# Attention followed by a ResMLP block: the first batch's pass takes the schedule of the later passes

## The chip, the cores and the metric

The kernel runs on one core of one Trainium2 chip. The metric is the device time of one execution in microseconds (us); the number given for a kernel is the median of its runs. PE is TensorE, DVE is VectorE, ACT is ScalarE, POOL is GpSimd and SP is SyncE; Pool and SP issue most of the DMAs, each on a queue of its own.

## What is computed

```python
B, Hq, Hkv, S, D = 8, 16, 4, 384, 64          # DM = Hq * D = 1024, DFF = 4096
k, v = repeat(k, 4), repeat(v, 4)             # four query heads share one k and v head
attn = softmax(q @ k.T / sqrt(D)) @ v         # [B, Hq, S, D]
x    = attn.transpose(0, 2, 1, 3).reshape(B, S, DM)
a1   = alpha1 * x + beta1
tok  = einsum('ts,bsd->btd', w_tok, a1)       # mixes the tokens of one batch
u    = x + lam * tok
a2   = alpha2 * u + beta2
ch   = relu(a2 @ w_ch1) @ w_ch2               # 1024 -> 4096 -> 1024
out  = u + lam * ch                           # float32, [8, 384, 1024]
```

Inputs and output are float32; the matmuls run in bf16 and accumulate in float32.

## The kernel before

The kernel goes through the eight batches one after the other. For each it has two kinds of work. The *side work* of a batch is everything up to `a2`: attention, token mixing, and the transposes that bring `a2` into `a2T`, which has the features on the partitions. The *pass* of a batch (`main`) is its MLP. During the pass of batch b, the side work of batch b + 1 is put between the matmuls of the MLP, so that PE always has something to do. The order on each engine is the order in which the program writes the instructions; nothing is reordered.

**The pass.** `main(b)` has two halves. The first half computes `hT`, 32 tiles of 128 hidden features (`nt` 0 to 31): each is eight matmuls `h` (L439, 128x128 by 384 columns, 385 in batch 0, where an extra column carries the bias) into one of two PSUM banks tagged "mm", and then an evacuation with ReLU, on ACT for even `nt` and on DVE for odd ones (L447, L449; in batch 0 a copy of the bias column goes ahead, L445). W1 does not stay in SBUF: it is loaded again in every pass in 16 chunks of two `nt` each (`load_w1`, L133, Pool's queue), into a ring of five buffers, so that the load of chunk c + 5 is issued when chunk c has been used. The second half computes six output tiles of 32 matmuls `ch` each (L474, 512 columns): first the three row tiles for the left 512 columns, then the three for the right ones. DVE multiplies by `lam` and adds the residual (L479, L480, two operations), and SP stores the tile (L481). W2 does stay in SBUF and is loaded once, in the first pass (`load_w2`, L138). The left half's first 16 `nt` are one load of 2048 KB that stands ahead of everything in `main`; the second quarter of W2, `nt` 16 to 31 of the left half, and the whole right half follow during the first pass.

**Yields and turns.** `main` is a generator. It yields in the middle and at the end of every `nt` of the first half (at the end only for the first four `nt` of batch 0, whose matmuls run ahead of the pass, in `h_part`), and after every four `ch` matmuls of the second half, 48 times. What the loop over the batches does at a yield is called a turn here.

In the passes of batches 1 to 6 `side(b + 1)` returns a table from a turn's number to what is issued there. Turns are counted from the last yield of the first half on, so turn 0 comes ahead of the first `ch` matmul. `scores3` computes three banks of scores (12 matmuls, L214) and their exponentials on ACT (L223); `av` multiplies by v for one pair of heads (18 matmuls, L257), after which DVE normalises and makes `a1` (L262, L263, L270, L272); `tok_flip` mixes tokens for the same 128 features (9 matmuls, L278), adds the residual and scales on DVE (L285, L289), and transposes the result into `a2T` with a DMA transpose on SP's queue (L301). Scores, av and tok share three PSUM slots of two banks each (`threes`). Turns 34 to 43 of these passes also carry the DMA transposes of the batch after: `flip_k` (L118) for `kT`, and `flip_q` (L122) for two pairs of heads at a time, four calls in all.

In the pass of batch 0, `side(1)` returns a list, and a rule on the time passed spreads its entries evenly over both halves. There the side work uses other PSUM pools: two slots for scores, one bank "av", one bank "tp". Scores are done in pairs of banks (`scores2`), and av in halves (`av_piece`). k and q of batch 1 are transposed on PE (`k_transpose`, L189; `q_transpose`, L200; DVE copies them out), and the rows of vectors h1, al2 and lam_t are spread over the partitions by matmuls (`spread`, L344, copied by ACT, L346) after DVE has split them into bf16 parts (`split`). The `a2` blocks of the first six pairs of heads go through DMA transposes, the last two through PE and ACT (L307, L310). At three quarters of the pass `flip_k(2)` and a single `flip_q(2)` for all heads are issued.

**Queues.** Pool's queue carries q, v, W1 and W2 in the order of the program; a load on it waits in its issue until the load eight places ahead has landed. Ahead of the first pass it has chunks 0 to 4 of W1, q and v of batch 1, and the first quarter of W2. SP's queue carries the stores, the loads of k and all DMA transposes, also in the order of the program.

The first pass before, as the loop sets it:

```python
for dt in main(b):
    t += dt
    if b == 0:
        ...
        if done < len(us) and done * t_all * 0.82 < len(us) * (t - t_all * 0.04):
            us[done]()
            done += 1
        if not flipped and t > t_all * 0.75:
            flipped = True
            flip_k(2)
            flip_q(2)
    elif t >= 2 * NNT * T_H:
        for f, *a in us.get(u, []):
            f(*a)
        u += 1
```

Of the kernel before, what the change touches and what calls it, by code (L numbers as in the profile page):

```python
# [12 lines left out]
def kernel(  # L13
# [157 lines left out]
    def side(b):  # L171
# [34 lines left out]
        def scores(i, later=False):  # L206
            sc = bank([P, 2, 4, P], "sc", "sc") if b < 2 else three()
            k = 4 * i
            while k < 4 * i + 4:
                n = min(4 * i + 4, k - k % NST + NST) - k  # L210
                p, sk, st = k // (NST * NST), k // NST % NST, k % NST
                for hh in range(2):
                    r = slice(hh * D, (hh + 1) * D)
                    nc.tensor.matmul(out=sc[:, hh, k % 4:k % 4 + n], lhsT=kT[r, sk, 2 * p // G, :],  # L214
                                     rhs=qT[r, p, st:st + n, :], start=True, stop=True)
                k += n

            def exp():
                if first:
                    e = hTf[:, i % 6 * 1024:(i % 6 + 1) * 1024].rearrange("p (h k s) -> p h k s", h=2, k=4)  # L220
                else:
                    e = sb.tile([P, 2, 4, P], bf, tag="es", name="es", bufs=EB)
                nc.scalar.activation(out=e, in_=sc, func=EXP, scale=scale_qk)  # L223
                ess[i] = e

            if later:
                late.append(exp)
            else:
                exp()

        def scores2(j):
            while late:
                late.pop(0)()
            scores(2 * j)
            scores(2 * j + 1, True)


# [4 lines left out]
        def av_piece(p, hh):  # L242
            while late and b < 2:
                late.pop(0)()
            if hh == 0:
                if b < 2:
                    avs[p] = bank([P, 2, NST, D1], "mm" if first else "av", "av")
                else:
                    avs[p] = three()[:, 0].rearrange("p k s -> p (k s)")[:, :2 * NST * D1].rearrange(
                        "p (h st d) -> p h st d", h=2, st=NST)  # L250
# [23 lines left out]
        def tok(p):  # L274
            ps = bank([P, NST, P], "mm" if first else "av", "tok") if b < 2 else three()[:, 0, :NST]
            for tt in range(NST):
# [14 lines left out]
        def a2_transpose(p):  # L291
            if first:
                ps = bank([P, NST, P], "tp" if p % 2 else "av", "ut")
                for tt in range(NST):
                    nc.tensor.matmul(out=ps[:, tt, :], lhsT=x[:, tt, cols(p)], rhs=ident_f, is_transpose=True,  # L295
                                     start=(tt == 0), stop=(tt == NST - 1), skip_group_check=True)
                nc.scalar.activation(out=a2T[:, p, :S], in_=ps.rearrange("p a b -> p (a b)"),
                                     func=mybir.ActivationFunctionType.Copy, scale=al2T[:, p:p + 1])
                return
            if b > 1 or p < 6:  # L300
                nc.sync.dma_start_transpose(  # L301
                    out=a2T[:, p, :S].rearrange("p (a s) -> p a s", a=NST),
                    in_=a2s[p].rearrange("p a d -> p (a d)"))
                return
            ps = tp_ps([P, NST, P])
            for tt in range(NST):
                nc.tensor.matmul(out=ps[:, tt, :], lhsT=a2s[p][:, tt, :], rhs=ident,  # L307
                                 is_transpose=True, start=(tt == 0), stop=(tt == NST - 1),
                                 skip_group_check=True)
            nc.scalar.copy(out=a2T[:, p, :S], in_=ps.rearrange("p a b -> p (a b)"))  # L310

# [42 lines left out]
        def av(p):  # L354
            av_piece(p, 0)
            av_piece(p, 1)
            if b > 1:
                while late:
                    late.pop(0)()

# [3 lines left out]

        if b > 1:

            return {0: [(scores3, 0)], 4: [(av, 0)], 6: [(scores3, 1)], 8: [(tok_flip, 0)], 11: [(av, 1)],
                    13: [(scores3, 2, True)], 15: [(av, 2)], 16: [(tok_flip, 1)], 18: [(tok_flip, 2)], 19: [(av, 3)],
                    21: [(scores3, 3)], 23: [(tok_flip, 3)], 25: [(av, 4)], 27: [(scores3, 4)], 29: [(tok_flip, 4)],
                    31: [(av, 5)], 33: [(scores3, 5, True)], 35: [(av, 6), (tok_flip, 5)], 37: [(av, 7)],  # L370
                    39: [(tok_flip, 6)], 41: [(tok_flip, 7)]}
        if not first:
            add(split, 2, 4)
            add(k_transpose, 0)
            add(q_transpose, 0, 2, "av")
            add(k_transpose, 2)
            add(q_transpose, 2, 2, "av")
            for j in range(NP + 4):
                if 1 < j < NP + 2:
                    add(av_piece, j - 2, 0)  # L380
                    add(av_piece, j - 2, 1)
                if j <= NP:
                    add(scores2, j)
                    if j in (1, 3):
                        add(q_transpose, 4 + 2 * (j // 2))
                if 2 < j < NP + 3:
                    add(tok, j - 3)
                if j > 3:
                    add(a2_transpose, j - 4)
                if j < 2:  # L390
                    for p in (4 * j, 4 * j + 2):
                        add(spread, (p, p + 1), (1, 3), "tp", "ACT")
                    add(spread, range(4 * j, 4 * j + 4), (3, 4), "tp", "ACT")
            return us
        add(k_transpose, 0, 1)
# [29 lines left out]

    T_H, T_C = 4 * S, 4 * 512

    def main(b):
# [3 lines left out]
        for c in range(NCH):  # L432
            w1 = w1_tiles.pop(b * NCH + c)
            for j in range(CW):
# [3 lines left out]
                for dt in range(0 if begun else NDT):  # L438
                    nc.tensor.matmul(out=ps[:, :n], lhsT=w1[:, dt, j * P:(j + 1) * P],  # L439
                                     rhs=a2T[:, dt, :n], start=(dt == 0), stop=(dt == NDT - 1))  # L440
                    if dt == 3:
                        yield T_H
                c1 = bias1[:, nt:nt + 1]
# [4 lines left out]
                else:  # L448
                    nc.vector.tensor_scalar(out=hT[:, nt, :], in0=ps[:, :S], scalar1=c1,  # L449
                                            scalar2=0.0, op0=ADD, op1=mybir.AluOpType.max)  # L450
                yield T_H

            if b or c + RING < NCH:
                load_w1(b * NCH + c + RING)
            if b == 0 and c in (3, 5, 7, 9):
                load_w2(0, 8 + c // 2 - 1, 16)
            if b == 0 and c == NCH - RING:
                for i in (6, 7):
                    load_w2(0, i, 8)
                for i in range(8):  # L460
# [5 lines left out]
        for dw in range(NDW):  # L466
            cs = slice(dw * 512, (dw + 1) * 512)
            for ms in range(NST):
# [3 lines left out]
                for lo, hi in ((0, 256), (256, 384), (384, 512)) if last else ((0, 512),):  # L472
                    for nt in range(NNT):
                        nc.tensor.matmul(out=ps[:, lo:hi], lhsT=hT[:, nt, ms * P:(ms + 1) * P],  # L474
                                         rhs=w2[:, nt, dw * 512 + lo:dw * 512 + hi], start=(nt == 0), stop=(nt == NNT - 1))
                        if nt % 4 == 3 and nt < NNT - 1:
                            yield T_C
                    c = slice(dw * 512 + lo, dw * 512 + hi)
                    nc.vector.tensor_tensor(out=o[:, lo:hi], in0=ps[:, lo:hi], in1=lam_t[:, c], op=MUL)  # L479
                    nc.vector.tensor_tensor(out=o[:, lo:hi], in0=o[:, lo:hi], in1=x[:, ms, c], op=ADD)  # L480
                    nc.sync.dma_start(out=out[b].rearrange("(p st) d -> p st d", st=NST)[:, ms, c], in_=o[:, lo:hi])  # L481
                yield T_C

    t_all = 2 * NNT * T_H + 8 * NST * NDW * T_C
    order = {mybir.EngineType.PE, mybir.EngineType.DVE, mybir.EngineType.Activation,
             mybir.EngineType.Pool, mybir.EngineType.SP}
    with tc.manual_schedule(engines=order):
# [99 lines left out]
        place_k(1, 0)  # L587
        place_k(1, 1)
        for b in range(B):
            us = side(b + 1) if b + 1 < B else {}  # L590
            half = False
            done, t = 0, 0
            if b == 0:
                load_k(2)
            elif b + 2 < B:
                for u, f, *a in ((1, load_k), (2, load_next), (34, flip_k), (36, flip_q, 0, 2), (37, flip_q, 2, 2),
                                 (42, flip_q, 4, 2), (43, flip_q, 6, 2)):
                    us.setdefault(u, []).append((f, b + 2, *a))
            flipped = False
            u = 0  # L600
            for dt in main(b):
                t += dt
                if b == 0:
                    half = not half
                    if late and half:
                        late.pop(0)()
                    if done < len(us) and done * t_all * 0.82 < len(us) * (t - t_all * 0.04):
                        us[done]()
                        done += 1
                    if not flipped and t > t_all * 0.75:  # L610
                        flipped = True
                        flip_k(2)
                        flip_q(2)
                elif t >= 2 * NNT * T_H:
                    for f, *a in us.get(u, []):
                        f(*a)
                    u += 1
            if b == 0:
                assert done == len(us)
                lead_banks.close()  # L620
                threes.append(ST(tc.psum_pool(name="threes", bufs=3)))
# [28 lines left out]
```

## Time and profile before

| | |
|---|---|
| median of 5 runs | 807.07 us (806.34 to 808.74) |
| profiled execution | 806.34 us |
| its span, first to last instruction | 804.6 us |
| busy share of the span | PE 99%, weight loads 56%, DVE 42%, ACT 28%, POOL 22% |
| granted TensorE clock | 1.00 |
| costliest lines on PE | ch L474 356.5 us, h L439 333.7 us |
| PE idle ahead of h L439 | 0.7 us in all |
| DMA | 112.97 MB moved, mean 140 GB/s |

The span is what the profile shows; 1.74 us of the execution lie around it. A busy PE is not PE at its peak, because matmuls are pipelined and their ends are modelled, so stages are compared by the distances between starts. Pass 0 begins with its first own h matmul at 39.45 us, pass 1 at 136.05, pass 2 at 233.43, pass 3 at 330.07; the passes after that follow at 96.65 us each.

### The profile page before, as it was taken

The numbers are of one execution on the slowest core, as the hardware profiler recorded it, in microseconds if no ns is written. First come the engines' busy times: TensorE is split into PE (matmuls) and PEld (weight loads), VectorE is DVE, ScalarE is ACT, GpSimd is POOL, SyncE is SP. The second block draws the span as 40 slices with busy tenths as digits, with TensorE's granted clock in tenths as the row PEclk, the third lists the DMA queues.
The fourth block names the chain that finished last, engine by engine and source line by source line (L and its number), as shares of the span: only waits on it lengthen the run. The fifth ranks groups of instructions, "written<-read, shape, count | busy, mean of one in ns | idle before, by whom it ended". The sixth has DMA issues, their size and how long they took to land.

```text
span 804.6 us, 14205 instructions
## 1 busy us (share of the span) xinstructions
PE 795.1 (99%) x6129; PEld 452.3 (56%) x6129; DVE 341.6 (42%) x669; ACT 227.9 (28%) x311; POOL 177.7 (22%) x232
## 2 busy tenths in 40 slices
PE   7999999999999999999999999999999999999997
PEld 4766554655556555565555655566555655556545
DVE  7655553225542256322662235622365225552122
ACT  6654310233402233123221234122421223402100
POOL 7135320332003500135002340033400330003000
PEclk9999999999999999999999999999999999999999
DMA  9999999999269972899439991599914994139511
GB/s 189 196 207 200 204 208 188 173 196 132 56 135 184 198 105 61 152 191 196 71 81 166 191 198 44 96 173 196 160 46 113 166 198 82 53 65 189 76 40 40
DMA packets 234030, 112.97 MB, mean 140 GB/s; under 512 B 83432, under 2 KB 227824, under 8 KB 233968
## 3 DMA queue, kind: packets, MB, share of 16 engines
q0 software_dynamic: 170736, 83.47, 78.7%
q1 hardware_dynamic: 62688, 28.20, 14.6%
q8 instruction: 48, 0.79, 0.4%
q10 hardware_dynamic: 544, 0.39, 0.2%
q14 instruction: 14, 0.11, 0.0%
HBM read 170.53 MB, written 12.58 MB: 228 GB/s over the span
## 4 chain that ended last, share of the span: by engine, by line
PE 88%; DMA 9%; DVE 2%; issue 0%; ACT 0%; SPq 0%; POOLq 0%
PE h L439 38%; PE ch L474 37%; DMA w<-in_moe_w_ch_dram 6%; PE sc L214 4%; PE sc L257 3%; PE sc L278 3%; DMA q_raw<-in_q_dram 2%; PE h L165 1%; PE tok L278 1%; PE av L257 1%; PE warm L492 0%; DMA a2T<-a 0%; PE ut L295 0%; PE tp L200 0%; DVE hT L561 0%
## 5 line engine op out<-in xcount | busy, mean ns | idle before, releaser
L474 PE MATMUL ch<-w,hT 128*128 128x512 bf16 (+2 forms) x1600 | 356.5, 371 | 0.9 <-DVE o L479 0.9
L439 PE MATMUL h<-a2T,w 128*128 128x384 bf16 (+1 forms) x2016 | 333.7, 326 | 0.7 <-DMA a2T<-a 0.4
L439 PEld LDWEIGHTS <-w 128*128 128x128 bf16 x2016 | 195.8, 98 | 130.3 <-issue 1.7
L133 POOL DMA_DIRECT2D w<-in_moe_w_ch_dram x128 | 112.3, 880 | 536.6 <-PE h L439 518.5
L474 PEld LDWEIGHTS <-hT 128*128 128x128 bf16 x1600 | 144.6, 98 | 153.0 <-issue 9.6
L223 ACT ACTIVATE es<-sc 128x1024 bf16<-128x1024 f32 x126 | 121.6, 1023 | 180.1 <-PE sc L214 172.7
L449 DVE TENSOR_SCALAR hT<-h,bias 128x384 bf16<-128x384 f32 x128 | 79.1, 618 | 217.6 <-PE h L439 217.0
L447 ACT ACTIVATE hT<-h,bias 128x384 bf16<-128x384 f32 x128 | 74.3, 580 | 305.9 <-PE h L439 305.4
L479 DVE TENSOR_TENSOR o<-ch,vecs 128x512 f32<-128x512 f32 (+2 forms) x50 | 33.3, 665 | 86.2 <-PE ch L474 81.5
L257 PEld LDWEIGHTS <-es 128*128 128x128 bf16 x1008 | 39.3, 97 | 14.3
L278 PEld LDWEIGHTS <-wtokT 128*128 128x128 bf16 x576 | 37.4, 98 | 13.6 <-DVE x L263 1.6
L214 PE MATMUL sc<-qT,kT 64*128 64x384 bf16 (+2 forms) x576 | 42.4, 271 | 0.1
L285 DVE TENSOR_TENSOR x<-sc,x 128x384 f32<-128x384 f32 x48 | 26.5, 552 | 32.2 <-PE sc L278 31.6
L262 DVE RECIPROCAL rinv<-sc 128x6 f32<-128x6 f32 x48 | 9.3, 193 | 66.1 <-PE sc L257 66.1
L214 PEld LDWEIGHTS <-kT 64*128 64x128 bf16 x576 | 21.3, 94 | 23.8 <-issue 17.6
L480 DVE TENSOR_TENSOR o<-o,x 128x512 f32<-128x512 f32 (+2 forms) x50 | 33.5, 670 | 1.7
L257 PE MATMUL sc<-v,es 128*128 128x65 bf16 x864 | 34.2, 193 | 0.0
L272 DVE TENSOR_TENSOR a<-a1f,vecs 128x384 bf16<-128x384 f32 x56 | 31.2, 557 | 2.2
L270 DVE TENSOR_TENSOR a1f<-x,vecs 128x384 f32<-128x384 f32 x56 | 31.2, 558 | 1.9
L289 DVE TENSOR_TENSOR a<-x,vecs 128x384 bf16<-128x384 f32 x56 | 31.2, 558 | 1.9
L278 PE MATMUL sc<-a,wtokT 128*128 128x128 bf16 x432 | 31.9, 219 | 0.0
L263 DVE TENSOR_TENSOR x<-sc,rinv 128x384 f32<-128x384 f32 x48 | 26.7, 557 | 1.6
(80 smaller groups left out, 228.6 us busy)
## 6 DMA issues: line engine op xcount, KB each, us to landing
w<-in_moe_w_ch_dram POOLq DMA_DIRECT2D x138, 512.0 KB, 8.8
out_dram<-o SPq DMA_DIRECT2D x47, 256.0 KB, 2.2
q_raw<-in_q_dram POOLq DMA_DIRECT2D x28, 192.0 KB, 8.2
kst<-in_k_dram SPq DMA_DIRECT2D x16, 192.0 KB, 3.4
w<-in_moe_w_ch_dram POOLq DMA_DIRECT2D x1, 2048.0 KB, 16.2
v<-in_v_dram POOLq DMA_DIRECT2D x24, 64.0 KB, 8.3
w<-in_moe_w_ch_dram POOLq DMA_DIRECT2D x4, 256.0 KB, 9.8
a2T<-a SPq DMA_TRANSPOSE x54, 2.3
```

What stands on the lines that cost most here:

```text
L133: nc.gpsimd.dma_start(out=t, in_=w1src[:, :, c * CW * P:(c + 1) * CW * P])
L214: nc.tensor.matmul(out=sc[:, hh, k % 4:k % 4 + n], lhsT=kT[r, sk, 2 * p // G, :], rhs=qT[r, p, st:st + n, :], start=True, stop=True)
L223: nc.scalar.activation(out=e, in_=sc, func=EXP, scale=scale_qk)
L257: nc.tensor.matmul(out=av[:, hh, sq, :], lhsT=ess[k // 4][:, m % 2, k % 4, :], rhs=vb[:, sk, hk, :], start=(sk == 0), stop=(sk == NST - 1))
L270: nc.vector.tensor_tensor(out=t, in0=x[:, :, cols(p)], in1=bc(g1, p), op=MUL)
L278: nc.tensor.matmul(out=ps[:, tt, :], lhsT=wtokT[:, st, tt * P:(tt + 1) * P], rhs=a1s[p][:, st, :], start=(st == 0), stop=(st == NST - 1 an ...
L439: nc.tensor.matmul(out=ps[:, :n], lhsT=w1[:, dt, j * P:(j + 1) * P], rhs=a2T[:, dt, :n], start=(dt == 0), stop=(dt == NDT - 1))
L447: nc.scalar.activation(out=hT[:, nt, :], in_=ps[:, :S], func=RELU, bias=c1)
L449: nc.vector.tensor_scalar(out=hT[:, nt, :], in0=ps[:, :S], scalar1=c1, scalar2=0.0, op0=ADD, op1=mybir.AluOpType.max)
L474: nc.tensor.matmul(out=ps[:, lo:hi], lhsT=hT[:, nt, ms * P:(ms + 1) * P], rhs=w2[:, nt, dw * 512 + lo:dw * 512 + hi], start=(nt == 0), sto ...
L479: nc.vector.tensor_tensor(out=o[:, lo:hi], in0=ps[:, lo:hi], in1=lam_t[:, c], op=MUL)
L480: nc.vector.tensor_tensor(out=o[:, lo:hi], in0=o[:, lo:hi], in1=x[:, ms, c], op=ADD)
```

## The change

The pass of batch 0 gets the table of turns that the later passes have.

- `side` now returns two tables for every batch after the first, one for each half of the pass. The table of the second half is the one of the later passes. For batch 1 alone the first half's table holds the preparation: `split`, `k_transpose` twice, `q_transpose` four times and `spread` six times. `scores2` and the pieces of av as separate entries go.
- `main` yields 0 in the first half and 1 in the second, and the loop counts the turns of each half from 0. Turn 0 of the second half is therefore at the first yield after four `ch` matmuls, in all passes.
- The pools of the first batch are closed, and `threes` is opened, at the first yield of the second half of pass 0, not after that pass.
- All eight `a2` blocks of batch 1 go through DMA transposes; the PE transposes L307 and the ACT copies L310 go.
- `flip_k(2)` and `flip_q(2)` become the turns 34, 36, 37, 42 and 43 of pass 0.
- W2's second quarter is no longer loaded between chunks of W1 (after chunks 3, 5, 7 and 9) with its rest behind them; it is loaded in eight pieces of 256 KB behind the last chunk of W1, ahead of the right half.

```diff
         def scores(i, later=False):
-            sc = bank([P, 2, 4, P], "sc", "sc") if b < 2 else three()
+            sc = bank([P, 2, 4, P], "sc", "sc") if first else three()
...
-            if b > 1 or p < 6:
-                nc.sync.dma_start_transpose(
-                    out=a2T[:, p, :S].rearrange("p (a s) -> p a s", a=NST),
-                    in_=a2s[p].rearrange("p a d -> p (a d)"))
-                return
-            ps = tp_ps([P, NST, P])
-            for tt in range(NST):
-                nc.tensor.matmul(out=ps[:, tt, :], lhsT=a2s[p][:, tt, :], rhs=ident,
-                                 is_transpose=True, start=(tt == 0), stop=(tt == NST - 1),
-                                 skip_group_check=True)
-            nc.scalar.copy(out=a2T[:, p, :S], in_=ps.rearrange("p a b -> p (a b)"))
+            nc.sync.dma_start_transpose(out=a2T[:, p, :S].rearrange("p (a s) -> p a s", a=NST),
+                                        in_=a2s[p].rearrange("p a d -> p (a d)"))
...
         if not first:
-            add(split, 2, 4)
-            add(k_transpose, 0)
-            add(q_transpose, 0, 2, "av")
-            add(k_transpose, 2)
-            add(q_transpose, 2, 2, "av")
-            for j in range(NP + 4):
...
-            return us
+
+            turns = {}
+            if b == 1:
+                turns = {1: [(split, 2, 4)], 4: [(k_transpose, 0)], 8: [(q_transpose, 0, 2, "av")], 12: [(k_transpose, 2)]}
+                for i in range(3):
+                    turns[16 + 4 * i] = [(q_transpose, 2 + 2 * i, 2, "av")]
+                for i in range(4):
+                    turns[29 + 4 * i] = [(spread, (2 * i, 2 * i + 1), (1, 3), "tp", "ACT")]
+                for i in range(2):
+                    turns[45 + 4 * i] = [(spread, range(4 * i, 4 * i + 4), (3, 4), "av", "ACT")]
+            return turns, {
+                0: [(scores3, 0)], 4: [(av, 0)], 6: [(scores3, 1)], 8: [(tok_flip, 0)], 11: [(av, 1)],
+                13: [(scores3, 2, True)], 15: [(av, 2)], 16: [(tok_flip, 1)], 18: [(tok_flip, 2)], 19: [(av, 3)],
+                21: [(scores3, 3)], 23: [(tok_flip, 3)], 25: [(av, 4)], 27: [(scores3, 4)], 29: [(tok_flip, 4)],
+                31: [(av, 5)], 33: [(scores3, 5, True)], 35: [(av, 6), (tok_flip, 5)], 37: [(av, 7)],
+                39: [(tok_flip, 6)], 41: [(tok_flip, 7)]}
...
-            if b == 0 and c in (3, 5, 7, 9):
-                load_w2(0, 8 + c // 2 - 1, 16)
             if b == 0 and c == NCH - RING:
-                for i in (6, 7):
-                    load_w2(0, i, 8)
+                for i in range(8, 16):
+                    load_w2(0, i, 16)
                 for i in range(8):
                     load_w2(1, i, 8)
...
+        load_k(2)
         for b in range(B):
-            us = side(b + 1) if b + 1 < B else {}
...
+            us = side(b + 1) if b + 1 < B else ({}, {})
+            if b + 2 < B:
                 for u, f, *a in ((1, load_k), (2, load_next), (34, flip_k), (36, flip_q, 0, 2), (37, flip_q, 2, 2),
-                                 (42, flip_q, 4, 2), (43, flip_q, 6, 2)):
-                    us.setdefault(u, []).append((f, b + 2, *a))
...
+                                 (42, flip_q, 4, 2), (43, flip_q, 6, 2))[2 * (b == 0):]:
+                    us[1].setdefault(u, []).append((f, b + 2, *a))
+            done = [0, 0]
+            for second in main(b):
+                if b == second - done[1] - 1 == 0:
+                    lead_banks.close()
+                    threes.append(ST(tc.psum_pool(name="threes", bufs=3)))
+                for f, *a in us[second].get(done[second], []):
+                    f(*a)
+                done[second] += 1
```

More of the change, by code (lines that the diff above doesn't have):

```diff
@@ L229, in scores @@
                 exp()
[L231 to L235, printed above, removed]
         def scores3(i, later=False):
@@ L242, in av_piece @@
         def av_piece(p, hh):
-            while late and b < 2:
-                late.pop(0)()
             if hh == 0:
-                if b < 2:
-                    avs[p] = bank([P, 2, NST, D1], "mm" if first else "av", "av")
+                if first:
+                    avs[p] = bank([P, 2, NST, D1], "mm", "av")
                 else:
@@ L274, in tok @@
         def tok(p):
-            ps = bank([P, NST, P], "mm" if first else "av", "tok") if b < 2 else three()[:, 0, :NST]
+            ps = bank([P, NST, P], "mm", "tok") if first else three()[:, 0, :NST]
             for tt in range(NST):
@@ L356, in av @@
             av_piece(p, 1)
-            if b > 1:
-                while late:
-                    late.pop(0)()
+            while late:
+                late.pop(0)()
         def tok_flip(p):
@@ L363, in tok_flip @@
             a2_transpose(p)
[L365 to L371, printed above, removed]
@@ L372, in side @@
-        if not first:
-            add(split, 2, 4)
-            add(k_transpose, 0)
-            add(q_transpose, 0, 2, "av")
-            add(k_transpose, 2)
-            add(q_transpose, 2, 2, "av")
-            for j in range(NP + 4):
[L379 to L393, printed above, removed]
-            return us
+        if not first:
+            turns = {}
[13 more added lines that the diff above has]
+                39: [(tok_flip, 6)], 41: [(tok_flip, 7)]}
@@ L423, in load_next @@
         load_v(b)
-    T_H, T_C = 4 * S, 4 * 512
     def main(b):
@@ L441, in main @@
                     if dt == 3:
-                        yield T_H
+                        yield 0
                 c1 = bias1[:, nt:nt + 1]
@@ L450, in main @@
                                             scalar2=0.0, op0=ADD, op1=mybir.AluOpType.max)
-                yield T_H
+                yield 0
             if b or c + RING < NCH:
                 load_w1(b * NCH + c + RING)
-            if b == 0 and c in (3, 5, 7, 9):
-                load_w2(0, 8 + c // 2 - 1, 16)
             if b == 0 and c == NCH - RING:
-                for i in (6, 7):
-                    load_w2(0, i, 8)
+                for i in range(8, 16):
+                    load_w2(0, i, 16)
                 for i in range(8):
@@ L476, in main @@
                         if nt % 4 == 3 and nt < NNT - 1:
-                            yield T_C
+                            yield 1
                     c = slice(dw * 512 + lo, dw * 512 + hi)
@@ L481, in main @@
                     nc.sync.dma_start(out=out[b].rearrange("(p st) d -> p st d", st=NST)[:, ms, c], in_=o[:, lo:hi])
-                yield T_C
-    t_all = 2 * NNT * T_H + 8 * NST * NDW * T_C
+                yield 1
     order = {mybir.EngineType.PE, mybir.EngineType.DVE, mybir.EngineType.Activation,
@@ L588 @@
         place_k(1, 1)
+        load_k(2)
         for b in range(B):
-            us = side(b + 1) if b + 1 < B else {}
[L591 to L595, printed above, removed]
-                for u, f, *a in ((1, load_k), (2, load_next), (34, flip_k), (36, flip_q, 0, 2), (37, flip_q, 2, 2),
-                                 (42, flip_q, 4, 2), (43, flip_q, 6, 2)):
-                    us.setdefault(u, []).append((f, b + 2, *a))
[L599 to L621, printed above, removed]
+            us = side(b + 1) if b + 1 < B else ({}, {})
+            if b + 2 < B:
+                for u, f, *a in ((1, load_k), (2, load_next), (34, flip_k), (36, flip_q, 0, 2), (37, flip_q, 2, 2),
+                                 (42, flip_q, 4, 2), (43, flip_q, 6, 2))[2 * (b == 0):]:
[8 more added lines that the diff above has]
+                done[second] += 1
 _INS = ['q', 'k', 'v', 'moe_alpha1', 'moe_beta1', 'moe_w_tok', 'moe_alpha2', 'moe_beta2', 'moe_w_ch1', 'moe_w_ch2', 'moe_lam']
```

## The prediction, made before the change ran

> **What bounds the kernel now.** I read the page first, then the busy times by stage, the time line of PE, the time line of SP, and the DMA view of short stretches. Pass b is the MLP of batch b; p0 to p7 are the eight a2T blocks that it needs.
>
> The page's 40 slices (20.1 us each), share of time that the DMA engines are busy, in tenths:
>
> ```profile
> DMA  9999999999269972899439991599914994139511
> ```
>
> For nine slices the DMA engines never rest; from slice 9 on they rest in every second half. The pass that changes is one where PE and DMA are both full. By stage (us, busy time of each engine, clock, DMA share, GB/s): pass 0, and the second half of pass 2.
>
> ```profile
> core 0: us, PE busy (x) PEld busy (x) DVE busy (x) ACT busy (x) POOL busy (x), PEclk, DMA share, GB/s
> 39.45:136.05 96.60, 96.29 (x764) 54.34 (x762) 47.16 (x101) 33.26 (x58) 31.47 (x41) 1.00 1.37 200
> ...
> 275.05:330.07 55.02, 55.02 (x481) 29.52 (x481) 30.32 (x59) 17.34 (x18) 7.88 (x12) 1.00 0.64 104
> ```
>
> A second half in threes takes 55.02 us with a DMA share of 0.64; in pass 0 it would run where the share is 1.37. PE's time line gives the price of an insertion, and the wait that ends pass 0:
>
> ```profile
> 46.57 0.50 PE L200 MATMUL tp<-ident,q_raw 128*128 128x128 bf16 x6
> 46.91 1.47 PE L439 MATMUL h<-a2T,w 128*128 128x385 bf16 x8
> ...
> 50.17 0.38 PE L344 MATMUL vec<-hT,stage 128*128 128x256 bf16 x2
> 50.39 1.47 PE L439 MATMUL h<-a2T,w 128*128 128x385 bf16 x8
> ...
> 137.44 2.76 PE L439 MATMUL h<-a2T,w 128*128 128x384 bf16 x16 [0.41 <-DMA a2T<-a]
> ```
>
> A turn of q shifts the next matmul by 0.34 us, a spread by 0.22. At 137.44 pass 1 has waited for p5. SP's queue shows why, first at the end of pass 0, then at the same place of pass 2 (start, time in the issue):
>
> ```profile
> 116.33 4.04 SPq L118 DMA_TRANSPOSE kT<-k  x1
> 120.56 13.02 SPq L122 DMA_TRANSPOSE qT<-q_raw  x1
> 133.68 0.53 SPq L481 DMA_DIRECT2D out_dram<-o  x1
> 134.26 1.20 SPq L301 DMA_TRANSPOSE a2T<-a  x1
> ```
>
> ```profile
> 315.72 1.46 SPq L118 DMA_TRANSPOSE kT<-k  x1
> 319.89 1.18 SPq L301 DMA_TRANSPOSE a2T<-a  x1
> 321.17 3.45 SPq L122 DMA_TRANSPOSE qT<-q_raw  x2
> 324.72 1.20 SPq L301 DMA_TRANSPOSE a2T<-a  x1
> 326.01 0.53 SPq L481 DMA_DIRECT2D out_dram<-o  x1
> 326.64 1.20 SPq L301 DMA_TRANSPOSE a2T<-a  x1
> ```
>
> Where the DMA engines are full, kT's issue takes 4.04 us for 1.46 and a quarter of q 13.02/4 = 3.25 for about 1.3. The queues from 123 to 131 us, then SP's alone from 134.2 to 137.2 (packets, MB):
>
> ```profile
> q0 software_dynamic: 1863, 0.94, 87.6%
> q1 hardware_dynamic: 1853, 0.47, 48.0%
> ```
>
> ```profile
> q1 hardware_dynamic: 2003, 0.91, 118.7%
> ```
>
> While Pool's queue has W1 to move, each queue gets 232 packets a us; SP's alone gets 668.
>
> **First half of pass 0.** PE after the change, from 39.45 us: 224 h matmuls at 0.1638 us (16 took 2.62, 39.45 to 42.07) are 36.7; two turns of k and four of q at 0.335 are 2.0; six spreads at 0.218 are 1.3: 40.0. split now comes after nt 1, not at nt 4; its DVE work (41.58 to 43.42, 1.84 us) and a copy of kT stand before the evacuation of nt 5, which then ends at about 44.7, while nt 7, which reuses that bank, could start at 44.05. I take 0.7 us (0 to 1.0; before, the same bank cost about 0.2, the 0.56 instead of 0.34 that the first turn of q took at 43.71). The half ends at 80.2.
>
> W1 is hidden, narrowly. Its sixth chunk, issued at 39.59, lands after 8.2 us, at 47.8; PE wants it (nt 10) at 48.3 to 49.0. After that a chunk every 2.65 us (0.524 MB at 198 GB/s) meets PE taking one every 2.62 plus a turn, so the margin grows. Price 0; if DMA ran 5% slower over those 8 us, 0.4. W2's second quarter: the last W1 chunk landed at 70.24 + 9.2 = 79.4 and comes 4 x 1.3 earlier, 74.2; the eight pieces behind it land at 75.5 to 84.7, and PE, entering the second half at 80.2, reaches the last of them after 30 x 0.2155 + 0.85 (a scores turn) + 0.56 (an av turn) = 7.9, at 88.1. Price 0, and the order on Pool's queue behind it is as before: the same bytes lead up to pass 1's first five W1 chunks.
>
> **Second half of pass 0.** It costs PE what it costs in pass 2: 275.05 to 329.91, 54.9 us, so pass 1 could start at 135.0. Before, its first matmul stood at 136.05, and the sixth at 137.44 instead of 136.86, an effective start of 136.63. On PE alone the change is worth 1.6 us: side work in threes is cheaper than in pairs, and two PE transposes (0.35) go.
>
> **What takes the gain.** p6 and p7 were PE turns copied by ACT, at 124.5 and 126.4; they become DMA transposes, and their place in SP's queue is behind kT and two quarters of q, whose issue under load is slow. From the time of the second half: kT at 80.2 + 40.3 = 120.5 (scores end there), issue to 124.5; p5 ready at 80.2 + 44.84 + 0.86 = 125.9, to 127.1; two quarters, the first partly into free queue space, to between 131.7 and 133.6; a store 0.53; p6 1.2 to 1.7; p7 issued between 133.5 and 136, landing 3.14 later (p5 of before, 134.26 to 137.40) or 2.3 (the median of all): 136 to 139. By packets (416 for a block of a2T, 1712 less 128 for kT without its store, about 768 for a quarter, about 140 for a store): p4 to p7, kT, two quarters and two stores are some 5,070; they start near 119 to 120.4, when W1 has 3,100 to 3,700 packets left; at 232 a us both run to about 134.5, then 1,400 to 1,900 remain at 668: 136.8, and the same count for before gives 135.6 where 137.4 was measured, 1.8 too early. So 136.8 to 138.6. I take 138.0, with 136 to 140 as ends. Pass 1 needs p7 at 135.0 + 7 x 0.1625 = 136.1: a wait of 1.9, an effective start of 136.9, 0.3 later than before.
>
> Beside the W1 stream the transposes move 0.47 MB in 8 us, 59 GB/s, by the row above. [...]
>
> **Behind it.** The other two quarters of q, a store and the next k load now move after p7, beside pass 1's W1 chunks. In pass 1 the sixteenth chunk, issued at 165.7, lands 9.3 later, at 175.0, and PE wants it at 175.8: 0.8 of cover, against about 1.2 us of added traffic (a quarter of q some 1.2 us each, less the store that left): 0.3 (0 to 1.0; no gain, because W1 makes PE wait nowhere in that half now).
>
> **All later passes.** Their turns were counted from the last yield of the first half, now from the first yield of the second: each comes four ch matmuls (0.86 us) later. PE's work is the same. Two covers shrink: a group's evacuation (0.72 + 0.61 us on DVE) now precedes the av 2 chain, so a1 of block 2 is ready some 0.1 us before tok 2; and p7 lands at about 329.6 for a need at 331.0. If tok 2 loses 0.1 in each of six passes, that is 0.6; if the cover holds, 0; a gain is excluded, since PE is busy for 55.02 of 55.02 us there. I take 0.1.
>
> Sum: +0.3 + 0.3 + 0.1 = +0.7 us. Against the profiled execution (span 804.6, 1.74 around it, 806.34): 807.0. The median of the runs is 0.73 above that execution: 807.07 + 0.7 = 807.8. A measurement of this kernel can tell about 0.2%, 1.6 us, from no change: 805.5 to 808.7 is "the same".
>
> **Rivals.**
> 1. The tie above: PE comes early and waits for transposes behind the same DMA work. For: 200 GB/s throughout pass 0, and the wait at 137.44 exists already. 805.9 to 809.2, centre 807.8. Chance 0.48 (0.43 of it same, 0.05 slower).
> 2. Faster: the transposes land in time, because two quarters of q (1,536 packets) move behind p7 while only 832 packets of a2T are added. PE then starts pass 1 at 135.0: 807.07 - 1.6 = 805.5; without the bank wait 804.8. Against: SP's issue times under load. Chance 0.19 (0.17 faster, 0.02 same).
> 3. Slower: SP's queue. If each issue takes its loaded time and p7 lands as p0 of pass 0 did (issued 76.45, 7.1 later), it lands at 140.5 to 142, and pass 1's W1 then arrives late by up to 1.0: +2.8 to +5, 809.9 to 812. It decides from a landing of about 139.3 on. Against: Pool's stream should be drained by then, as at 134.74 before. Chance 0.28.
> 4. Slower by a missing cover: without side work PE runs onto W1's landings in pass 0's first half, or later passes lose 0.3 each: +1.7 to 2.5, 809.2. Against: 0.5 to 1.2 us of margin at the sixth chunk, growing. Chance 0.05.
>
> **Numbers.** Faster 0.17, same 0.45, slower 0.05 + 0.28 + 0.05 = 0.38. The range runs from the middle of rival 2, 805.3, to the lower part of rival 3, 810.6; outside it lie some 0.08 below and 0.12 above. Rival 1's own range is 805.9 to 809.2.
>
> **What would show it.** In the profile after: the first half ends near 80.2 with no wait for w; L307 is gone; pass 1's first h matmul starts near 135 and its eighth waits near 138 on a2T; SP's q issues in pass 0 take over 2.5 us each; passes 2 to 6 stay at 96.6. I am wrong if no matmul of pass 1's nt 0 waits (rival 2), if that wait passes 3.2 us (rival 3), or if PE waits for w in pass 0 or for a1 in later passes (rival 4).

## The result, and the profile after

The changed kernel takes 806.10 us (median of 25 runs, 804.93 to 809.91), the kernel before, run beside it, 806.97 us (45 runs, 805.91 to 811.51). The ratio is 0.9990, with a 95% interval of 0.9981 to 0.9999: a gain of 0.9 us at the edge of what these runs can tell, where 0.7 us of loss was forecast. The time lies inside the forecast range and inside the band that was called "the same", but the kernel moved the other way.

The profiled execution of the changed kernel took 806.11 us, with a span of 804.3 us. First the page's DMA row:

```profile
DMA  9999999999269972999439991399914995139611
```

The same slices at the start are full; both rows show ten of them, not the nine that the prediction counted. By stage, pass 0 and the second half of pass 2 (columns as before):

```profile
core 0: us, PE busy (x) PEld busy (x) DVE busy (x) ACT busy (x) POOL busy (x), PEclk, DMA share, GB/s
39.45:135.43 95.98, 95.14 (x758) 54.51 (x756) 47.24 (x101) 31.79 (x56) 32.62 (x43) 1.00 1.37 198
...
274.93:329.97 55.04, 55.04 (x481) 29.44 (x480) 30.47 (x59) 17.34 (x18) 7.87 (x12) 1.00 0.64 103
```

Pass 0 now takes 95.98 us on PE, 0.62 less; a later second half takes 55.04. PE's time line at the places that the prediction named, the bank of nt 7, the end of the first half and the start of pass 1:

```profile
43.39 0.82 PE L406 MATMUL h<-a2T,w 128*128 128x385 bf16 x4
45.05 2.13 PE L406 MATMUL h<-a2T,w 128*128 128x385 bf16 x12 [0.84 <-DVE hT L416]
...
80.39 1.03 PE L439 MATMUL ch<-w,hT 128*128 128x512 bf16 x4
...
135.43 1.14 PE L406 MATMUL h<-a2T,w 128*128 128x384 bf16 x6
137.49 3.75 PE L406 MATMUL h<-a2T,w 128*128 128x384 bf16 x21 [0.92 <-DMA a2T<-a]
```

There is no wait for W1 in the first half, and pass 1 comes 0.62 us earlier and waits longer: after six matmuls, for p6, 0.92 us; p7 holds one more matmul up, to 137.83. SP's queue at the end of pass 0:

```profile
120.87 3.66 SPq L118 DMA_TRANSPOSE kT<-k  x1
126.28 1.53 SPq L292 DMA_TRANSPOSE a2T<-a  x1
127.90 5.36 SPq L122 DMA_TRANSPOSE qT<-q_raw  x2
133.35 0.53 SPq L446 DMA_DIRECT2D out_dram<-o  x1
133.98 2.52 SPq L292 DMA_TRANSPOSE a2T<-a  x2
```

The two quarters of q hold SP for 5.36 us (the first issue takes 1.83, the second 3.44), and p6 and p7 are issued behind them, as the prediction had it (p7 at about 135.3, between the 133.5 and 136 of its working).

To compare executions I call the time from pass 1's first h matmul to its first ch matmul, less what the same stretch takes in pass 2 (42.46 us before, where turn 0's scores stand ahead of the first ch, and 41.60 after), the loss at pass 1's start. All starts are those of the PE time line: pass 2's first h matmul stands at 233.27 before, and the 233.43 given above is the modelled end of the matmul ahead of it. The loss is 0.57 us in the first profile of before and 1.26 in that of after.

### The profile page after: what moved, and what is told of

It is laid out like the page before. It is cut to its first block, busy times and chain, and to the rows that moved or that the text cites. A ratio compares the mean times of both kernels' runs of the same rounds, so it can differ in the third digit from the quotient of the medians.

```text
span 804.3 us, 14218 instructions
## 1 busy us (share of the span) xinstructions
PE 794.2 (99%) x6123; PEld 452.6 (56%) x6123; DVE 342.8 (43%) x669; ACT 226.4 (28%) x309; POOL 178.8 (22%) x234
## 4 chain that ended last, share of the span: by engine, by line
PE 96%; DVE 2%; SPq 1%; DMA 0%; issue 0%; ACT 0%
PE ch L439 41%; PE h L406 40%; PE sc L214 4%; PE sc L249 4%; PE sc L270 3%; SPq L122 1%; PE h L165 1%; PE tok L270 1%; PE av L249 0%; PE warm L456 0%; DMA a2T<-a 0%; PE ut L287 0%; PE tp L200 0%; DVE x L255 0%; DVE hT L525 0%
## 5 line engine op out<-in xcount | busy, mean ns | idle before, releaser
L249 PE MATMUL sc<-v,es 128*128 128x65 bf16 x1008 | 39.8, 193 | 0.0
L277 DVE TENSOR_TENSOR x<-sc,x 128x384 f32<-128x384 f32 x56 | 30.9, 552 | 20.0 <-PE sc L270 20.0
L270 PE MATMUL sc<-a,wtokT 128*128 128x128 bf16 x504 | 37.3, 219 | 0.0
L255 DVE TENSOR_TENSOR x<-sc,rinv 128x384 f32<-128x384 f32 x56 | 31.2, 557 | 1.9
```

Of the source, the lines that this page charges most:

```text
L249: nc.tensor.matmul(out=av[:, hh, sq, :], lhsT=ess[k // 4][:, m % 2, k % 4, :], rhs=vb[:, sk, hk, :], start=(sk == 0), stop=(sk == NST - 1))
L255: nc.vector.tensor_tensor(out=x[:, :, cols(p)].rearrange("p st (h d) -> p h st d", h=2), in0=av[:, :, :, :D], in1=rinv.to_broadcast([P, 2, ...
L270: nc.tensor.matmul(out=ps[:, tt, :], lhsT=wtokT[:, st, tt * P:(tt + 1) * P], rhs=a1s[p][:, st, :], start=(st == 0), stop=(st == NST - 1 an ...
```

## The experiments

Two theories. *Landing* (the *tie* of the first expectations): pass 1 starts when its last a2T blocks have landed, and these stand behind other transposes and the W1 stream. *PE*: the shorter work on PE made the gain, and the wait is a detail. Every ratio is to the kernel before, run beside the experiment; its medians in the three sets of runs were 806.85, 807.02 and 807.14 us.

**The two kernels once more.** No edit.

> The kernel before once more, to see how far one execution's profile stands for the median. If pass 1's wait for a2T is the same in every execution, pass 1's first undisturbed h matmul stands at 136.6 us again and the ratio is 1.000 within 0.001. If the DMA-full lead-in varies from execution to execution, this profile shows another wait at the start of pass 1 (0.4 us in the first profile), larger if its time is above 806.3.

> The changed kernel once more. Tie theory (the transposes behind the full DMA queues set pass 1's start in both kernels): ratio 0.999 to 1.000, pass 1's seventh h matmul waits until 137 to 138 us. PE theory (the shorter PE work is what made it faster): ratio 0.998 to 0.999, and the wait of about 1 us at pass 1's start is absent in some executions.

Before again: ratio 1.0005 (0.9994 to 1.0015), no difference, as it must be. But its profiled execution took 808.60 us, and its PE time line at pass 1's start reads:

```profile
134.95 0.98 PE L439 MATMUL h<-a2T,w 128*128 128x384 bf16 x5
138.03 4.26 PE L439 MATMUL h<-a2T,w 128*128 128x384 bf16 x15 [2.11 <-DMA a2T<-a]
```

Here the lead-in was 1.1 us faster, PE came 1.1 us earlier, and p5 landed no earlier: 138.03 after 137.44. The wait is 2.11 us instead of 0.41. And after it the clock falls (stages of the same execution, columns as above):

```profile
134.00:138.00 4.00, 1.93 (x11) 0.88 (x9) 1.39 (x2) 0.00 (x0) 0.00 (x0) 1.00 1.24 253
138.00:141.40 3.40, 3.37 (x11) 1.57 (x11) 0.00 (x0) 0.58 (x1) 0.00 (x0) 0.51 0.55 185
```

PEclk is 0.51 from 138.0 to 141.4 and 0.66 from 138 to 143, which makes 3.4 us at half the clock. Half of that, an estimated 1.7 us, comes on top of the wait. The loss is 3.93 us. After again: 806.02 us, ratio 0.9994 (0.9983 to 1.0004), a wait of 1.21 us until 137.79, full clock (a mean of 1.000 over the execution), loss 1.66.

**split_later.** PE is made to come earlier, and nothing else is touched:

```diff
-                turns = {1: [(split, 2, 4)], 4: [(k_transpose, 0)], ...
+                turns = {4: [(k_transpose, 0)], ...
+                turns[17], turns[21] = [(split, 2, 4, 0)], [(split, 2, 4, 1)]
```

> The changed kernel with split moved from the end of nt 1 to the ends of nt 10 and nt 12, so that DVE evacuates nt 5 in time. Both theories: PE's wait of 0.85 us before nt 7 goes, the first half of pass 0 ends near 79.6 instead of 80.4. Tie theory: the a2T transposes land where they did or at most 0.5 us earlier, pass 1's wait grows by what PE gained, the total against the changed kernel is -0.5 to 0 us. PE theory: -0.8 us.

The bank wait is gone, the first half ends at 79.37, pass 1's first matmul stands at 134.42, 1.0 us earlier. The kernel is *slower* than the changed one: 808.28 us for the 806.02 of a_again in the same set. Against before the ratio is 1.0013 (0.9999 to 1.0028).

```profile
134.42 1.14 PE L407 MATMUL h<-a2T,w 128*128 128x384 bf16 x6
138.93 7.29 PE L407 MATMUL h<-a2T,w 128*128 128x384 bf16 x32 [3.37 <-DMA a2T<-a]
```

A wait of 3.37 us, then 3.4 us at half the clock (PEclk 0.50; columns as above):

```profile
139.98:143.40 3.42, 3.42 (x13) 1.66 (x11) 0.62 (x1) 0.30 (x1) 0.88 (x1) 0.50 0.65 192
```

Of its 12 executions three took 805.1 to 805.5 us, nine 807.8 to 810.9, and those nine have a mean clock of 0.998 or less; of the changed kernel's 25 runs five do (807.90 to 809.91). In the profile the wait grew by 2.45 us, of which 1.0 is PE's earlier arrival; the rest is a landing at 138.93 instead of 137.49, a little later than the 138.83 of a_third below. Neither theory had foreseen that less work costs time; the PE theory falls, and the landing theory needs the clock.

**q_late.** The blocks land earlier, and PE's work is the same:

```diff
-                for u, f, *a in (..., (34, flip_k), (36, flip_q, 0, 2), (37, flip_q, 2, 2),
+                u0, u1 = (42, 42) if b == 0 else (36, 37)
+                for u, f, *a in (..., (34, flip_k), (u0, flip_q, 0, 2), (u1, flip_q, 2, 2),
```

> The changed kernel with the first two quarters of q's transposes of pass 0 moved from turns 36 and 37 to turn 42, behind p6 and p7. Tie theory: 1,536 packets fewer ahead of p6 and p7 (2.3 us at 668 packets a us), so they land before 136.4, pass 1's wait of about 1 us is gone, and of that 0 to 0.6 us is given back where the quarters move beside pass 1's W1 chunks: -1.2 to -0.6 us against the changed kernel. PE theory: no change (within 0.2 us).

805.31 us, ratio 0.9974 (0.9963 to 0.9985), 0.8 less than the changed kernel (0.7 less than a_again in the same set). SP now issues p6 and p7 ahead of q, from 130.56 on:

```profile
130.56 2.48 SPq L292 DMA_TRANSPOSE a2T<-a  x2
133.13 5.48 SPq L122 DMA_TRANSPOSE qT<-q_raw  x4
```

Pass 1 starts where it did, and does not wait:

```profile
135.45 6.84 PE L406 MATMUL h<-a2T,w 128*128 128x384 bf16 x40
```

**pe_last2.** The wait is taken away in the other manner, by the transposes on PE that the change removed:

```diff
+            if b > 1 or p < 6:
                 nc.sync.dma_start_transpose(out=a2T[:, p, :S]...
+                return
+            ps = three()[:, 0].bitcast(bf)[:, :NST]
+            for tt in range(NST):
+                nc.tensor.matmul(out=ps[:, tt, :P], lhsT=a2s[p][:, tt, :], rhs=ident, is_transpose=True, ...)
+            nc.scalar.copy(out=a2T[:, p, :S].rearrange("p (a s) -> p a s", a=NST), in_=ps[:, :, :P])
...
-                39: [(tok_flip, 6)], 41: [(tok_flip, 7)]}
+                **({39: [(tok, 6)], 41: [(tok, 7)], 42: [(a2_transpose, 6)], 44: [(a2_transpose, 7)]} if b == 1 else
+                   {39: [(tok_flip, 6)], 41: [(tok_flip, 7)]})}
```

> The changed kernel with the last two a2 blocks of batch 1 again transposed on PE and copied by ACT (turns 42 and 44). Landing theory: no wait for a2T at pass 1's start, its first h matmul at 135.8 us (0.35 of PE work more), -0.9 us against the changed kernel in its median, more against executions with a longer wait. PE theory: +0.4 us.

805.32 us, ratio 0.9973 (0.9963 to 0.9984). Pass 1 starts at 135.77, 0.34 later than in the changed kernel, without a wait, and the kernel is 0.8 us faster. Ten of its 12 executions lie between 805.26 and 805.53: with the wait, most of the spread goes too.

```profile
135.77 6.50 PE L415 MATMUL h<-a2T,w 128*128 128x384 bf16 x39
```

**w2_mid.** W2's second quarter between W1's chunks, as before the change:

```diff
+            if b == 0 and c in (3, 5, 7, 9):
+                load_w2(0, 8 + c // 2 - 1, 16)
             if b == 0 and c == NCH - RING:
-                for i in range(8, 16):
-                    load_w2(0, i, 16)
+                for i in (6, 7):
+                    load_w2(0, i, 8)
```

> The changed kernel with W2's second quarter loaded as before (a piece after W1 chunks 3, 5, 7 and 9, the rest in two loads). Landing theory (pass 1 starts when its last a2T blocks land, whenever PE comes): PE waits for w in the first half of pass 0, 1 to 3 us in all, comes to pass 1 that much later and waits for a2T that much less: 0 to +1 us against the changed kernel (806.1). PE theory: +1 to +3 us. If W2's place is idle detail: no wait for w, no change.

806.38 us, ratio 0.9991 (0.9980 to 1.0001), 0.3 more than the changed kernel: not told apart by the intervals. PE waits for the last chunk of W1, comes to pass 1 at 136.64, 1.2 us later, and waits 0.77 us for p7:

```profile
78.97 2.79 PE L406 MATMUL h<-a2T,w 128*128 128x385 bf16 x16 [0.90 <-DMA w<-in_moe_w_ch_dram]
```

So W2's place does spare PE 1.2 us in pass 0. How much of that the wait takes back is not settled: in the medians 0.3 us of it is left, in the two profiles 0.9 (the last matmul ends at 802.02 instead of 801.14, with a loss of 0.93 instead of 1.26). It also means that PE's gain in the changed kernel hangs on W2's place: without it PE comes to pass 1 0.6 us later than in the kernel before (136.64 for 136.05), not earlier.

**both, b_q_late.** split_later with q_late; and the kernel before with its one q transpose behind p5:

```diff
-            flipped = False
+            flipped = flipped_q = False
...
                         flip_k(2)
+                    if flipped and not flipped_q and t > t_all * 0.92:
+                        flipped_q = True
                         flip_q(2)
```

> split later and the two quarters of q behind p7 together. Landing theory with the clock (a wait of about 2 us or more at pass 1's start is followed by 3.4 us at half the clock, a shorter one is not): PE comes to pass 1 at 134.4 instead of 135.4, p6 and p7 land at 135.5 to 136.7, wait 0 to 1 us and no half clock: -1.0 to 0 us against q_late (805.3), 804.3 to 805.3. If the wait passes 2 us: +1 us or more.

> The kernel before with its single q transpose of pass 0 issued behind p5 (at 0.92 of the pass, not 0.75). Landing theory: the wait for p5 (0.4 to 2.1 us in two profiles) is gone and no execution shows the half clock at 138 us; 3,070 packets move beside pass 1's W1 chunks, which may cost up to 1 us there: -1.5 to +0.3 us against before. PE theory: no change.

both: 804.79 us, ratio 0.9971 (0.9959 to 0.9984). In its profile the lead-in was again 1.1 us faster, and the wait is

```profile
136.25 6.05 PE L407 MATMUL h<-a2T,w 128*128 128x384 bf16 x36 [1.72 <-DMA a2T<-a]
```

with full clock behind it (PEclk 1.00 from 134 to 143 us), longer than the 0 to 1 us expected because PE came 1.1 us earlier still; one of its 12 executions took 807.71, at a clock of 0.998. b_q_late: 805.79 us, ratio 0.9980 (0.9971 to 0.9990), no wait and no loss at pass 1's start (h at 136.38; the lead-in of this profile was 0.3 us slower). The kernel before had this wait too, and a reordering of SP's queue alone, without the change, is worth 1.2 us of its median.

**best, best_qlate.** pe_last2 with the split of split_later; the same with the quarters of q late.

> PE transposes for the last two blocks (as in pe_last2) and split late (as in split_later). Landing theory: nothing at pass 1's start hangs on blocks that land late, so here the 0.85 us of the bank wait do count, which they did not in split_later: 805.3 - 0.9 = 804.4, no half clock, a narrow spread; slower than pe_last2 only if p5 lands after 135.6. PE theory: the same 804.4; the two differ in split_later, not here.

> As best, with the two quarters of q of pass 0 at turn 42 besides. Landing theory: p5 stands ahead of those quarters already, so nothing is gained: 804.4 within 0.3, or up to 0.5 more where the quarters move beside pass 1's W1.

best: 804.32 us (6 runs, 804.28 to 804.46), ratio 0.9961 (0.9948 to 0.9975); pass 1 starts at 134.74, without a wait. The edit that made the changed kernel 2 us slower makes this one 1.0 us faster than pe_last2, and pass 1 starts 1.0 us earlier in its profile. best_qlate: 804.34 us (803.22 to 805.65), 0.9962 (0.9948 to 0.9977): nothing more to gain, and a wider spread. best beats both kernels, before by 2.8 us.

**A third profile of each.** No edit.

> The changed kernel, a third profile. Landing theory with the clock: wait at pass 1's start between 0.5 and 2 us with full clock, or over 2 us followed by 3.4 us at half the clock; the time follows from it: 805.2 plus the wait, plus 1.7 where the clock falls.

> The kernel before, a third profile: the same rule. With a wait near 0.4 us 806.3, with 1 to 1.5 us about 807, over 2 us with the half clock 808.5 or more.

After: 809.35 us. PE came at 135.44 as always, the block only at 138.83, and then the clock fell: PEclk is 1.00 from 138.8 to 140.0 us, 0.51 from 140.0 to 143.5 and 1.00 again from there to 150, some 3.4 us at half the clock:

```profile
138.83 3.60 PE L406 MATMUL h<-a2T,w 128*128 128x384 bf16 x13 [2.25 <-DMA a2T<-a]
```

Before: 806.89 us, a wait of 0.66 us, full clock (PEclk 1.00 from 134 to 143 us).

## Why the prediction was wrong, step by step

| profile | pass 1's first h at | wait for a2T | half clock | loss | execution |
|---|---|---|---|---|---|
| before | 136.05 | 0.41 | no | 0.57 | 806.34 |
| b_third | 136.34 | 0.66 | no | 0.81 | 806.89 |
| w2_mid | 136.64 | 0.77 | no | 0.93 | 806.98 |
| after | 135.43 | 0.92 | no | 1.26 | 806.11 |
| a_again | 135.44 | 1.21 | no | 1.66 | 806.65 |
| both | 133.39 | 1.72 | no | 1.92 | 804.74 |
| b_again | 134.95 | 2.11 | 3.4 us | 3.93 | 808.60 |
| a_third | 135.44 | 2.25 | 3.4 us | 4.32 | 809.35 |
| split_later | 134.42 | 3.37 | 3.4 us | 5.46 | 809.30 |

- **The mechanism was right.** Rival 1 described the profile: PE early (135.43 for 135.0), q's two issues 5.36 us together, 1.83 and 3.44 rather than over 2.5 each, p7 arriving at 137.83 for 138.0, an effective start of 137.83 - 7 x 0.1625 = 136.69 for 136.9, against 136.63 before. In the pair of profiles the last matmul of the whole kernel ends 0.06 us *later* after the change (801.14 for 801.08).
- **The step that failed is the reference.** The sum was made against one execution of before, whose loss of 0.57 us is the smallest of the three profiles of before, and the 0.73 us up to the median were carried over to the changed kernel as if they belonged to every execution. They were part of the same loss. Without it the execution of before would have been 806.34 - 0.57 = 805.8 us; b_q_late, which has no loss, has a median of 805.79. So the median of before holds a loss of about 1.2 us; this is inferred, since the profiled execution of b_q_late took 806.19. For after, 806.11 - 1.26 = 804.85, and the median of 806.10 holds 1.25. The median losses are alike, and what is left between the kernels is PE's 0.62 us and the next item. The forecast's wait of 1.9 for after was set against 0.58 for before; against 1.2, and with the measured 1.25, that +0.3 becomes -0.6 (PE's -0.62 and 1.25 less 1.2).
- **A term was missing.** From the last matmul to the end of the span it is 3.49 us before and 3.20 after. At the end SP waits for ten DMA semaphores, in the same order in both traces, some 0.06 us each where the transfer had landed (the first eight after the change from 802.20 to 802.63). The wait for the last store ended at 803.31 and 803.37, but its semaphore is the fourth of the ten before and the ninth after, because the change issues five more DMAs on SP's queue (157 for 152: two blocks of a2T, three more calls for q) and in both traces SP's DMAs take eight semaphores in turn. Five waits fewer behind the landing are 0.3 us. In the profiles of before, b_again, b_third and b_q_late this tail is 3.49 to 3.51, in those with the five DMAs more 3.18 to 3.20, and in pe_last2, best and best_qlate, which have two of the five fewer, 3.31 to 3.32.
- **Two small terms were zero.** W1 in pass 1 (+0.3): none of the loss lies behind p7. The shift of the turns in later passes (+0.1): pass 2 takes 96.64 us in both, and from its start to the last matmul of the kernel it is 567.81 us in both.
- **The gain on PE** was 0.62, not 1.05: the bank wait was 0.84 beside a first half that ended at 80.39 (for 80.2), and the second half took 55.04, not 54.86. The prediction had measured that 54.86 from the modelled end of an h matmul (275.05) to the start of another (329.91), so it came out 0.18 us short. The gain of 0.62 itself is steady: pass 0 takes 96.60 us on PE in all three profiles of before and 95.98 or 95.99 in those of after.
- **Rival 2** had the sign, with a mechanism that no profile of the changed kernel shows (the wait is there in all three). **Rival 3** set its point at a landing of 139.3 by price alone; the half clock makes it decide earlier, at 138.83 in a_third. **Rival 4** fell: no wait for W1 and none for a1.

The arithmetic of the medians, PE 0.62 and the tail 0.3 with equal losses, gives 0.9 us and fits; it is inferred from three profiles of each kernel, not shown for every run. Why the last block lands anywhere from 137.5 to 138.8 in the same kernel was not tried, but the traces show what goes with it. The last packet that Pool's queue moved ahead of pass 1 (the same 41,008 packets up to there) started at 134.46, 134.90 and 136.18 us in the three profiles of after, and PE went on at 137.49, 137.79 and 138.83; in those of before it was 134.39, 134.99 and 135.46, and 137.44, 137.97 and 138.03. So the block lands later where the stream of weights ends later; why that stream ends later stays open, as does why the lead-in was 1.1 us faster in two profiles.

## What to carry to other kernels

Before an edit that shortens one engine's work, ask what that engine will meet when it arrives early; here a wait of 0.92 us became one of 3.37, and with the half clock behind it the loss was larger than the work saved. Put transfers that someone waits for soon ahead of those that nobody needs yet, above all where the DMA engines are full; that order alone was worth 0.8 us in q_late and 1.2 us in b_q_late. And one profiled execution is a poor base for a forecast of a microsecond where its own wait varies by several: take a second one, or an edit that removes the wait, and compare those.

## What the runs showed of the hardware

In the profiles of the table a wait of PE longer than 2 us was followed by some 3.4 us at half the clock. Waits of 0.41, 0.66, 0.77, 0.92, 1.21 and 1.72 us were not followed by it; 2.11, 2.25 and 3.37 were, and the half clock started between 0 and 1.2 us after PE had resumed: PEclk is 0.51 from 138.0 to 141.4 us in b_again, 0.51 from 140.0 to 143.5 in a_third and 0.50 from 139.98 to 143.40 in split_later. No profile has a wait between 1.72 and 2.11 us, and whether the length of the wait is all that counts was not shown.

From 123 to 131 us of the first profile of before, Pool's queue moved 1863 packets and SP's 1853, about the same number, although Pool's were twice as large (0.94 MB for 0.47). In the first profile of after, q's two quarters beside the stream of weights took 5.36 us of issue, for the 2.57 that two take in pass 2 of the same profile. That they were held to the pace of that stream is an inference from these two readings.
